# Two-piece loads (120 and 8 rows) for ten early tiles, and a new order of all operations, in a gated linear attention and MLP kernel

## The chip, the cores and the metric

The kernel runs on one core of a Trainium2 chip. The metric is the device time of one execution in microseconds (us). The kernel before takes 165.41 us, the median of three runs between 165.22 and 166.08.

## The reference

The inputs q, k, v and alpha are float32 of shape (4, 8, 768, 48): four batches, eight heads, 768 steps, 48 columns. A recurrence runs over the steps, and its output, with the heads side by side, goes through a mixer with a residual and an MLP with a residual:

```
state = alpha[t][:, None] * state + outer(k[t], v[t])     # for each batch and head
x[t]  = q[t] @ state                                       # x: (4, 768, 384)
u     = x + transpose(transpose(x) @ U @ V)                # U: 768 x 32, V: 32 x 768
out   = u + relu(u @ w_ch1) @ w_ch2                        # w_ch1: 384 x 1536, w_ch2: 1536 x 384
```

## The kernel before

**Attention.** The recurrence is computed in chunks of 128 steps, six for each batch. The logarithm of alpha (written `lt`, on ACT) is summed over the steps by matmuls ("cumulative matmuls", L343 and the lines behind it), exponentiated into `aa` and `ai`, and multiplied into q and k (`rq`, `rk`, L364 and L530, on DVE or POOL). `rv` is a cast of v (L258 on ACT, L262 on POOL). TensorE transposes rk and rq (L377, L543), forms scores (L404, L568), which are masked into `pm` (L415, L578), carries the state on (`st`; L438 are matmuls of rk with rv), and computes the chunk's output into `xb`.

**Two kinds of units.** In batch 0 all six units, and in batch 1 the first four, are *pair* units: two units (halves, of four heads each) share a block of 256 steps. Their tiles are loaded with two neighbouring steps in each partition (L304). The other chunks are loaded by L311. One unit needs four tiles: alpha, k, q and v. A tile is named here by its input, batch (b0), block and half. Every tile of an input, and every tile of 128 x 384 of the weights, has 128 rows and 192 KB.

**Mixer and MLP.** `stage_mix` multiplies by U and V and adds (`ub`) and transposes (`uT`). `mlp1` (L732 on PE, relu on ACT at L742 or on DVE at L744) and `mlp2` (L755 on PE, adding at L762 on DVE, output transfer at L763) follow for each batch. Weights come through `weight` (transfer L277, cast L258 or L262).

**Order.** `Plan.add` records operations with the engines that may run each. `Plan.run` plays them by `TABLE`, three characters for each operation: two for its number and one for its engine (P TensorE, A ACT, D DVE, G POOL, S the queue of SP). `++X` stands for some filler matmuls (L251, on a tile of zeros, into a bank that nothing reads). `SLOTS` names for each operation's new buffers which slot of their pool they take. The order is thus one list, written out beforehand: each engine runs its operations in the list's order and waits only for what they need. All transfers, the outputs' included, are issued on SP, in the list's order, from the `io` pool of 36 tiles. They take eight semaphores in rotation, so transfer n waits until transfer n − 8 has landed. The change's places are these:

```
op.fn({"P": "PE", "A": "ACT", "D": "DVE", "G": "POOL", "S": "SP"}[table[n + 2]])
...
P.add({"SP": 545.0}, lambda e: nc.sync.dma_start(flat(t), src), w=[t])      # weight
```

In the order before, the last tile of batch 0 is v of block 2, half 0, transfer number 25 counting from 0. Sixteen fillers run: 11 ahead of the first cumulative matmul, then 2, 2 and 1 between the first units' cumulative matmuls.

Of the kernel before, what the change touches and what calls it, by code (L numbers as in the profile page):

```python
# [13 lines left out]

CODE = "ABCDEFGHIJKLMNOPQRSTUVWXYZabcdefghijklmnopqrstuvwxyz0123456789+-"
TABLE = """
A8SA4SBESCuA++LCwPBISCYAA+SCyAA9SDbAC1DCaPDyAA5SCxAA7S++CD0PDdPCbAA-SCZGDeAC0DA6SD3ACzAC2PCcACeDC4DCdAC3PC5DBGS++CCnPCoD
BASC6PD2ADfACvACpPDgACfDD1ABMSCgPChPBFSCiAC8DCjDDEABHSBBSDiGCqDC9PC+D++BDkPDGPBDSC-PEHACkPC7DEJPDmABCSBQSDhDDBPBOSDHADAD
DcGBNSDIAClDDJADjPDKDDTPBKSEKABJSDCAELADFGDMPDqPDlDABSDDAEMADLGBPSBLSBSSCmDDrPDOABUSBRSGLADUPDnPDsDDtPDVDDNPDpDAASDoDEOG
DuDDWPGNPCrPDPAGOAEQPDQPGQAENDCsDBTSCtAEPPD5GDXDBVSESADRDDvPBXSERAAeSD7PETPD4GDwADSDGPAD9ADYPADGDxDD6PEVDBYSEWPEBPEIGAGP  # L20
DZDGSGDaDEUDBcSDzAD8AAEPECPAKSAcSAaSGRGEXPD+PGhAEDDAMSGUPAFAGjPAHAEYDEZPGTPGMGACGEADD-DGWAEEPEbDGkAGlAGmAGaPGnGGVDEFAEaD
EGDAfGEcPAISAQSGbDALGGiABWSGXPEdPEeABfSAdGAOSGwPGcDGZDEiPGxDElPEjPAbGEmPGYDErPEsPEkAEoPANGE7PASSEuPGyDE5PBdSHOAGpPAJGEfP
EpPBbSE8DEgPEvPEtDBZSG3AEqAARGHQPAUSExPEnDEzPBaSEhDEwABeSAgSG5PG7AAYSFrPAPGAWSFRPEyDBkSE-PBgSGrAFTPE0DE6DATGFpPHRAAmSFBP
AkSFAAFSDG6ABiSFqAFnPGoDHPGAiSE1PFCAE9PBhSGzDG8AE2DFUDE3PGqPHUDFPPBlSFoAGdGBmSFfPG9GFbPFsAE+DHTAE4DHWPHSAFVPFZPHYDAVGHdP
FQAAuSG4AFWDFgAHGPFcAGsAGePFaDBjSHHDG+GAXGGtPGfDHeDGvDGgDFDPFdPFEAAsSG-PAZAFHPFIAFeDHAPFXPHVDHXPGuDHCAHIGH7AHBDFhPAoSFLP
H9PFYAFMAAqSHfDHlABnSHgDFiAAnGH+AHZDHJDA0SAySFNPHDPAlGAwSA2SFOAHaPBoSHnPHqAAhGH-AFlPHEDFJPBrSHpABwSHoAHFDFjPFFPHrAAjGHbD
HLPFmDHcDHKDG0PFkAHhDHiPHMAHtGIADFGAHNAHvPHjDG1DIBDGGPICPBsSHsGHkAHuPIDPFKDG2AFyPHxAHmGIEAHwDIFAHyPIGPBvSH0DF8PFtPHzDIHD
H1PAvAApGH2DArAAtGGBPH8ABpSH3DH5PFzPIIDF9PA1AAxAA3AH4GIJPGHPH6DGCPIKDAzGILPBySJtAFuPIMAF0PIPPIQDINPGDPB0SIODBxSITPF1DKWA
IVPB8SGIPIRPF2SIWDBtSIUDIbPJvPIcDFvPIZPIaDBqSIXPISAKYPKBAIYDGJDKcABuSKZAF+PKDPIdPKHAJwAGKSFwDBzSCASIeDKbAKrAInPIhPIoDCQS
KaAIfPJyAJ0GB2SIxPKGAJxAGEDIpPIiDKEAIlPJuGB+SIgAF-DKdDIyDKFAB9SKeDJzAImDI-PJ2PKIDI3PB1SKtPIzPLVAI0DB3SKxAJHPB4SI4ACESJFP  # L30
FxSJ4DJAAKCGB5SJ1DB6SJ9PJGDJ+DIjPIqAKuAIkDKJGKRPJ3PIrPJBPLXPKwAKvAKLPKXGKSDNHAI9PB7SJ5DJIDLYAIsDIvPLZAKKPKfPKhDJCAI5PKgP
KNDI+DKMAJNPJOAKTDI6AItPI1PKmPJJPKiDI2AIwAJLPKnDIuDJMACCSI7PJ6PKjPKOPKPDJKAI8ALbGF3PLAACDSKsAKQDJDPOaANJPJ7DKlDF4PB-SKyG
NbAF5PNNAK0PLCPKkDK7PJUPLFALEAJ8DLGAKUPK2DKzDLDAKVDLdPCBSJEDKoGJVPNdPLaGCMSNLANgAJWPGFSNKALIGNfALcPK1PLfDCFSNhALHGJjPLWG
JXDNMALBGKpPJkPK8DK3ACISJ-PNPGLeDNeAGASLJPKqAF6DLKPJPPLgPKADK4PLLDCGSK5DCUSLMALNPOFALODCOSJQPJRPJePLiDLQPLPDJfPF7SK9GJlP
CSSK6DCHSNOGNIANQPLhDNRPJmDLRDOcPLSGOgACRSOHPLTPJSDK+PCNSNjGOfANTDJgPNSALUDOKALjPNiGJZPK-ALkDJTSJaPOeANUPCLSNVDLlPJoPNwA
OIALmAOMGJhDNXPOdALtPOJACXSNWDJpPLvPLpPL1POLANyPLuDNYDLwDN0ACJSLnPJqPLxPLoDONGLqDLzPL2DNkPOiGL0DJnSOvANcALrPJrDJbPLyANZP
NlPLsAN2ANaDNrPNnACVSMJPL3PCKSMFPNzAOxPMKDNsDN1AMHPMNPMGDL4AOhDCPSJcDOzAL-POOPNmAMODMLPMIAMTPMAAMVPOyAOjPCTSMUDNtGL7PNxG
MMDJdSOPPL9PN3DORDOQAL5PO0GL8DOAPMhPMnPMWAOlAL6AN5PMRPOkPCWSMXPL+DOBDN4DNoPOCGMSAOmDMiAMoAOwGOSPOUDOTDOGGMBPMPPMlPO1GMYA
MDPN6PMQANpDN7AO2PMjPMCDMEAJiSObGOVPOYPNqDO4DOWDOXGMZPO3PMkDMmAN8AOqPMaDMuPOrDOZANuPOnPOoDO5AO6POsDN9PN+DMvPMdPMwPMzPN-D
OpDMbPO8DMfPO7DM4PMeDO9PMgAO+AODPNvAOEAOtPM0PMxDOuDNCPO-PMcAM5PM6PPAAPPPPNPPJPJYSPODM1PPHPMpPPQDPKDNDPPRPM2DPBPPIDPCDM9P  # L40
PLPPSDMqPPDPM+PMrPPMDPEDJsSPFPNEPMySM7DP3PPxPPvPPGDMsDPwDPZPPaDPTPP4APlPPpPPdPPjPPUDM3SPeDPVPPyDPfPNFDPWAQBPM-PPXPP-PPkD
PtPPgDPmDPqAP5PPrPPYDPbPQCAPsAP6DP9PPuAPhPQAAPcDPzPPnPP+ANADPiAQIPP7PQSPQDPP1PMtSQNPP8AQEPPoDP0AQXPQFPP2DQGDM8SQJPQKPQcP
QdPNGSQYPQLDQHSQePQOPQZPQMSNBSQPPQfDQaDQgSQTPQUPQQDQVDQbSQRSQWS
"""
SLOTS = """
ABCAADBEAFCABAGAHCDBIACAJABEBBACFAKGAALEBCABDBAMFGNBABBOPCDCBBFQAGADCRSCEBTBCUBBCCDFVCWAADGECBAXYZCAabCBDACDECBGFADBDECD
BcACdAAFBeBfDEAABBFCBBgGAEDAhBCFijACCBBBBEAAGFDACCBCCACEFDADCDACEAGAFGBCAAECFDAGBHEBAIAHCJAKCBLDGMNOFCPEQCRDSBHGATAUABVC
BDWDGXAAFADYZCBHBEBBGCAEaEDCDHBbBCFGBABDHcAGDBAHABBAGdFDeDAfBCBAhgAEBijFHACCAGCEBCCAABADFGCAHBCDCBFDDHACCBBAAGDEFECHABDA
GAGEADFHCBEBDFIFABEJDKCEFLCBDABDMBFCAACQPCBABNBCBATBCDDCGERABAUAAHCCSFEBOCBWVGCCXBYCCAACEHDGCBFDBAAZDBEAHBACDBBGBHBFACGA
bDCBFEHGABACdBDBHCBcDABGCEFACBCCCCGaDCAeADAABBDAfCGABCHBBhFBABECDBCAHFBiAjCEDCBgHCEAACBDADDAFCCDCGAEFCDAABDACDGGBEBACAAC  # L50
DAEABHFGCCBBEEDAHEBBEFACGDBAHCIBFJGBDABCBCHDAHFCGEACCMABCHDBBBFDEGHAACBKFACDEDABCBAAGHBAFCCCHDDAGBBCFEDBHACAGBBDFDEBAAEB
CGFDGADHDBCGAABDGCCAEABCBGEBABFCDGBFCBDECHFGBDECGBCFDHAECBADBDABC
"""


# [21 lines left out]
class Plan:  # L77
# [40 lines left out]
    def run(self, table, slots):  # L118
        nxt = iter(slots)
        for n in range(0, len(table), 3):  # L120
            if table[n : n + 2] == "++":
                for _ in range(CODE.index(table[n + 2])):
                    self.warm()
                continue
            op = self.ops[CODE.index(table[n]) * len(CODE) + CODE.index(table[n + 1])]
            for b in op.bufs:
                if b.slot is None:
                    b.slot = b.pool.slots[CODE.index(next(nxt))]
            op.fn({"P": "PE", "A": "ACT", "D": "DVE", "G": "POOL", "S": "SP"}[table[n + 2]])


def mm(*cols):
# [4 lines left out]
def kernel(  # L137
# [12 lines left out]
    nc = tc.nc  # L150
    B, H, S, D = q.shape
# [21 lines left out]
    P = Plan()  # L173
# [82 lines left out]
    def copy(eng, dst, src):  # L256
        if eng == "ACT":
            nc.scalar.copy(dst, src)  # L258
        elif eng == "DVE":
            nc.vector.tensor_copy(dst, src)  # L260
        else:
            nc.gpsimd.tensor_copy(dst, src)  # L262

    def small():
# [4 lines left out]
        for i in range(2):  # L269
# [2 lines left out]
            P.add({"PE": mm(TW)}, lambda e, vb=vb, sl=sl: nc.tensor.matmul(vb()[:, 0:TW], lhsT=sel.rearrange("r a b -> r (a b)"), rhs=v_bf[:, sl], start=True, stop=True), r=["v_bf"], w=[vb], mode="V")  # L272
            P.add({"DVE": 470, "ACT": 390}, lambda e, vb=vb, sl=sl: copy(e, vm_sb[:, sl], vb()[:, 0:TW]), r=[vb], w=[("vm", i)])

    def weight(dst, src, key, engs):
        t = Buf(io)
        P.add({"SP": 545.0}, lambda e: nc.sync.dma_start(flat(t), src), w=[t])  # L277
        P.add(engs, lambda e: copy(e, dst, flat(t)), r=[t], w=[key])

    def flat(t):  # L280
        return t().rearrange("p h d -> p (h d)")

    def weights1():
# [11 lines left out]
    def paired(b, c):  # L295
        return c // 2 < PAIRS[b]

    def stage_loads(b):
        def load(t, src, c):
            if paired(b, c):  # L300
                hs, sl = slice((c % 2) * HP, (c % 2 + 1) * HP), slice((c // 2) * 2 * C, (c // 2 + 1) * 2 * C)
                P.add(
                    {"SP": 775.0},
                    lambda e: nc.sync.dma_start(  # L304
                        t().rearrange("p (h j) d -> p h (j d)", j=2), src[b, hs, sl, :].rearrange("h (p j) d -> p h (j d)", j=2)
                    ),
                    w=[t],
                )
# [508 lines left out]
```

## Time and profile before

| | us |
|---|---|
| median of three runs | 165.41 |
| profiled execution, whole | 167.33 |
| its span (first to last instruction) | 165.5 |
| around the span | 1.83 |
| PE busy | 156.8 (95%), 1810 matmuls |
| DVE, ACT, POOL busy | 121.5, 90.5, 54.0 |
| transfers on SP | 146, 28.5 MB |

The profile is one execution, and its times are microseconds from the span's start. "PE" is TensorE's matmuls, "PEld" its weight loads, which run beside them. SPq is the time that SP's queue takes to issue a transfer, waiting for a semaphore included. A row of the chain or of the waits names an instruction by output and line, and behind "<-" what released it last.

### The profile page before, as it was taken

How to read it: one execution, taken by the hardware profiler on the slowest of the kernel's cores; microseconds unless marked ns; L12 is line 12 of the kernel's file. 1: busy time of each engine (PE TensorE's matmuls, PEld its weight loads, DVE VectorE, ACT ScalarE, POOL GpSimd, SP SyncE). 2: the span in 40 equal slices, each digit the busy share in tenths (PEclk: the TensorE clock that was granted, in tenths of full speed). 3: DMA queues.
4: the chain of work that ended last, by engine and by line, in shares of the span. 5: the costliest groups of instructions: out<-in, count | busy, mean ns of one | idle time of the engine just before them, and what ended most of it. 6: DMA issues, size and time to landing. Idle time of an engine off the chain costs nothing.

```text
span 165.5 us, 4676 instructions
## 1 busy us (share of the span) xinstructions
PE 156.8 (95%) x1810; PEld 103.0 (62%) x1810; DVE 121.5 (73%) x271; ACT 90.5 (55%) x225; POOL 54.0 (33%) x88
## 2 busy tenths in 40 slices
PE   7897959999999999999999999999999999999991
PEld 2455737666767656667677675766777566566660
DVE  6198957988999817999697887887988285752241
ACT  4598847679497363885876354994724201342000
POOL 7032848439445310422717453364320000000000
PEclk9999996999999999999999999999999999999999
DMA  5999979999989979999999999966000012100133
GB/s 126 279 289 267 255 170 247 279 324 310 260 174 269 286 141 216 195 228 204 199 218 233 210 246 197 223 142 190 0 4 29 18 53 95 46 1 4 48 143 143
DMA packets 87126, 28.81 MB, mean 174 GB/s; under 512 B 80928, under 2 KB 87072, under 8 KB 87104
## 3 DMA queue, kind: packets, MB, share of 16 engines
q1 hardware_dynamic: 87104, 28.52, 69.7%
q8 instruction: 14, 0.23, 0.6%
q14 instruction: 8, 0.07, 0.1%
HBM read 23.79 MB, written 4.72 MB: 172 GB/s over the span
## 4 chain that ended last, share of the span: by engine, by line
PE 78%; SPq 9%; DMA 4%; DVE 3%; issue 1%; ACT 1%; POOL 1%; ACTq 0%
PE ps L755 28%; PE ps L732 27%; SPq L304 9%; DMA io<-in_v_dram 4%; PE ps L543 3%; PE ps L680 2%; PE ps L568 2%; PE ps L701 2%; PE ps L635 2%; PE ps L377 1%; PE ps L510 1%; PE ps L630 1%; PE ps L650 1%; PE ps L591 1%; DVE pm L415 1%
## 5 line engine op out<-in xcount | busy, mean ns | idle before, releaser
L755 PE MATMUL ps<-w_sb,h1t 128*128 128x384 bf16 x288 | 54.0, 326 | 0.0
L732 PE MATMUL ps<-uT,w_sb 128*128 128x384 bf16 x288 | 53.0, 326 | 0.0
L742 ACT ACTIVATE h1t<-ps 128x384 bf16<-128x384 f32 x52 | 23.7, 496 | 28.8 <-PE ps L732 28.3
L755 PEld LDWEIGHTS <-h1t 128*128 128x128 bf16 x288 | 26.2, 97 | 16.2 <-issue 1.2
L732 PEld LDWEIGHTS <-w_sb 128*128 128x128 bf16 x288 | 26.5, 98 | 15.0 <-POOL w_sb L262 0.2
L744 DVE TENSOR_SCALAR h1t<-ps 128x384 bf16<-128x384 f32 x44 | 23.4, 551 | 7.7 <-PE ps L732 7.6
L578 DVE TENSOR_TENSOR pm<-ps,maskc 128x512 bf16<-128x512 f32 x28 | 17.6, 684 | 4.8 <-PE ps L568 3.3
L681 DVE TENSOR_TENSOR ub<-xb,ps 128x384 bf16<-128x384 bf16 x24 | 12.3, 549 | 8.2 <-PE ps L680 8.2
L762 DVE TENSOR_TENSOR ou<-ub,ps 128x384 f32<-128x384 bf16 x24 | 13.1, 549 | 7.0 <-PE ps L755 6.8
L415 DVE TENSOR_TENSOR pm<-ps,maskp 128x512 bf16<-128x512 f32 x20 | 13.3, 685 | 0.2
L262 POOL CAST w_sb<-io 128x384 bf16<-128x384 f32 x18 | 9.1, 517 | 11.5 <-DMA io<-in_moe_w_ch_dram 11.4
L530 POOL TENSOR_TENSOR rk<-io,ai 128x384 bf16<-128x384 f32 x9 | 8.2, 913 | 13.6 <-DMA io<-in_alpha_dram 9.1
L262 POOL CAST rv<-io 128x384 bf16<-128x384 f32 x16 | 8.4, 532 | 12.1 <-DMA io<-in_v_dram 11.1
L530 POOL TENSOR_TENSOR rq<-io,aa 128x384 bf16<-128x384 f32 x9 | 8.5, 952 | 9.3 <-DMA io<-in_q_dram 5.7
L260 DVE CAST xb<-ps 128x192 bf16<-128x192 f32 (+1 forms) x19 | 8.1, 437 | 3.4 <-PE ps L635 2.7
L602 POOL TENSOR_TENSOR st<-sm,tot 128x384 bf16<-128x384 f32 x7 | 6.1, 865 | 13.9 <-DVE sm L618 6.6
L258 ACT COPY qt<-ps 128x512 bf16<-128x512 bf16 x14 | 9.3, 668 | 1.8 <-PE ps L543 1.0
L523 ACT ACTIVATE tot<-ps,off 128x4 f32<-128x4 f32 x22 | 5.7, 278 | 8.2 <-PE ps L512 7.8
L503 ACT ACTIVATE lt<-io 128x384 bf16<-128x384 f32 x14 | 7.4, 530 | 1.6 <-DMA io<-in_alpha_dram 1.6
L258 ACT COPY kt<-ps 128x512 bf16<-128x512 bf16 x12 | 7.1, 590 | 1.1 <-PE ps L377 0.8
L521 ACT ACTIVATE aa<-ps 128x384 bf16<-128x384 f32 x14 | 7.0, 508 | 1.1 <-PE ps L512 1.1
L364 POOL TENSOR_TENSOR rq<-io,aa 128x384 bf16<-128x384 f32 x6 | 5.8, 970 | 5.0 <-ACT rv L258 2.3
(116 smaller groups left out, 252.5 us busy)
## 6 DMA issues: line engine op xcount, KB each, us to landing
io<-in_alpha_dram SPq DMA_DIRECT2D x24, 192.0 KB, 4.2
io<-in_q_dram SPq DMA_DIRECT2D x24, 192.0 KB, 3.7
io<-in_k_dram SPq DMA_DIRECT2D x24, 192.0 KB, 4.1
io<-in_v_dram SPq DMA_DIRECT2D x24, 192.0 KB, 4.0
io<-in_moe_w_ch_dram SPq DMA_DIRECT2D x24, 192.0 KB, 4.6
out_dram<-ou SPq DMA_DIRECT2D x24, 192.0 KB, 2.2
v_in<-in_moe_V_dram SPq DMA_DIRECT2D x1, 96.0 KB, 3.7
u_in<-in_moe_U_dram SPq DMA_DIRECT2D x1, 96.0 KB, 4.8
```

Of the source, the lines that this page charges most:

```text
L258: nc.scalar.copy(dst, src)
L262: nc.gpsimd.tensor_copy(dst, src)
L304: lambda e: nc.sync.dma_start(t().rearrange("p (h j) d -> p h (j d)", j=2), src[b, hs, sl, :].rearrange("h (p j) d -> p h (j d)", j=2)),
L415: nc.vector.tensor_tensor(dst, s2, maskp.to_broadcast([C, 2, 2, C]), op=ALU.mult)
L530: eng.tensor_tensor(dst()[:, :, 0:D], a(), x(), op=ALU.mult)
L578: nc.vector.tensor_tensor(pm()[:, :, par, :], s2, maskc.to_broadcast([C, HP, C]), op=ALU.mult)
L681: P.add({"DVE": 465}, lambda e, c=c, hb=hb: nc.vector.tensor_tensor(ub()[:, c, :], xb()[:, c, :], hb()[:, 0:DM], op=ALU.add), r=[hb] + xk( ...
L732: nc.tensor.matmul(hb()[:, 0:TW], lhsT=w1_sb[:, ct, jt * 128 : (jt + 1) * 128], rhs=u_half(uT, ct, tt, b in QUEUE_U), start=(ct == 0), sto ...
L742: nc.scalar.activation(dst, hb()[:, 0:TW], AF.Relu)
L744: nc.vector.tensor_scalar_max(dst, hb()[:, 0:TW], 0.0)
L755: nc.tensor.matmul(hb()[:, 0:DM], lhsT=h1()[:, jt, c * C : (c + 1) * C], rhs=w2_sb[:, jt, :], start=(jt == 0), stop=(jt == NJ - 1),)
L762: P.add({"DVE": 468}, lambda e: nc.vector.tensor_tensor(ou(), ub()[:, c, :], hb()[:, 0:DM], op=ALU.add), r=[hb, (ub, c)], w=[ou])
```

## The change

`Plan.run` knows two engine letters more: "Q" (ACT) and "X". A load or weight whose letter is X is issued as two transfers, one of rows 0 to 119 and one of rows 120 to 127, one behind the other on SP; with S it is one transfer of 128 rows, as before. `TABLE` and `SLOTS` are replaced throughout.

```diff
-            op.fn({"P": "PE", "A": "ACT", "D": "DVE", "G": "POOL", "S": "SP"}[table[n + 2]])
+            op.fn({"P": "PE", "A": "ACT", "D": "DVE", "G": "POOL", "S": "SP", "Q": "ACT", "X": "SX"}[table[n + 2]])
...
+    def parts(e, dst, src):
+
+        cuts = (0, 120, 128) if e == "SX" else (0, 128)
+        for lo, hi in zip(cuts, cuts[1:]):
+            nc.sync.dma_start(dst[lo:hi], src[lo:hi])
+
     def weight(dst, src, key, engs):
         t = Buf(io)
-        P.add({"SP": 545.0}, lambda e: nc.sync.dma_start(flat(t), src), w=[t])
+        P.add({"SP": 545.0, "SX": 545.0}, lambda e: parts(e, flat(t), src), w=[t])
...
                 P.add(
-                    {"SP": 775.0},
-                    lambda e: nc.sync.dma_start(
-                        t().rearrange("p (h j) d -> p h (j d)", j=2), src[b, hs, sl, :].rearrange("h (p j) d -> p h (j d)", j=2)
+                    {"SP": 775.0, "SX": 775.0},
+                    lambda e: parts(
+                        e, t().rearrange("p (h j) d -> p h (j d)", j=2), src[b, hs, sl, :].rearrange("h (p j) d -> p h (j d)", j=2)
                     ),
```

What the new table holds, counted from it:

| | before | after |
|---|---|---|
| operations on PE, DVE, ACT, POOL | 369, 245, 224, 73 | 369, 234, 236, 72 |
| loads and outputs in one piece, in two | 146, 0 | 136, 10 |
| transfers on SP | 146 | 156 |
| place of the last b0 tile (v, block 2, half 0) | 25 | 31 |
| fillers ahead of the first cumulative matmul | 11 | 8 |
| fillers behind it | 2, 2, 1 | 1, 3, 1, 2, 1 |

The ten tiles in two pieces, in the order of their issue: q b0 block 1 half 0, v b0 block 1 half 1, q b1 block 0 half 0, a tile of w_ch1, alpha b1 block 1 half 0, another tile of w_ch1, q b1 block 0 half 1, q b1 block 1 half 0, a tile of w_ch2, and v b1 block 1 half 1. Lines behind `parts` stand six lines further down.

More of the change, by code (lines that the diff above doesn't have):

```diff
@@ L16 @@
 TABLE = """
[L17 to L40, printed above, removed]
@@ L41 @@
-PLPPSDMqPPDPM+PMrPPMDPEDJsSPFPNEPMySM7DP3PPxPPvPPGDMsDPwDPZPPaDPTPP4APlPPpPPdPPjPPUDM3SPeDPVPPyDPfPNFDPWAQBPM-PPXPP-PPkD
-PtPPgDPmDPqAP5PPrPPYDPbPQCAPsAP6DP9PPuAPhPQAAPcDPzPPnPP+ANADPiAQIPP7PQSPQDPP1PMtSQNPP8AQEPPoDP0AQXPQFPP2DQGDM8SQJPQKPQcP
-QdPNGSQYPQLDQHSQePQOPQZPQMSNBSQPPQfDQaDQgSQTPQUPQQDQVDQbSQRSQWS
+A4SCYABMSBESBASBGSA8SA7SDbADEAA6S++ICaPEHABBS++BDdPCuAA5SCdABQS++DDGPA+SA9SBDSBISA-SCcABFSABSEJPCbAAYSDfABCXBHXDHABNSCfD
+BUSBOSBJSBRSDKDDIABKSBcSBPSDiGCwPBLSBSXCZGAUSBTS++BChPAaSAASCxACjD++CDkPAcSDgACeDDeAAKXGLABYX++BCgPCzADFGCyAAeSBgSDJADmD
@@ new lines @@
+C0DCnPCoDDMPEKACiAAWSASSC2PC1GCpPELADyACkPDhGADGDLGCqDDODCvAAIXDTPDUPBZSCmDD0PEMADVDC9PClDAQSAMSBVSGNPDcGC+DDWPC4AD1AAOS
+C3PC-PBWXDXDD2ADjPC5DBkSAGPAEPDADGOAAqSENGAZAD3AC6PAHDEOGDNPDqPA2SD4GAFAC7DDlAD5GGhADrPDPADnPGRGBeSAgSGPADsDEIGDtPBXSBdS
+C8DDuDGjPAkSGQAGlADpDGSGAmSCrPGMGBaXAwSEQPDoDESADQPDRDD6PCtAEPPAiSD8DBiSGkAA0SDSDAbGDvPERAD7PGTPACGGmADwDDxDEWPCsAETPAoX
+D9AAuSAdGAfGGVDHOAEVDDBPDYPDCAAsSEXPEUDBbSD+PDzADaADZAAJGARGHQPDDAEYDGUPAySEBPD-DGoGGWAEADECPEZPEDDBfXEaDATGGaPEbAEEPGXP
+HRAGbDEGDEFAGcDEcPEdPEfPErPHTAEiPAVAGZDEeAHSAGYDEuPG3AEoPEgPEsPElPEpPEjPAPGEvPEmPE1PEhDG5PEqABhSEkAEwDE3PGdDEnAG8AEtDBmS
@@ new lines @@
+EzPExPHlAFRPFTPArGAhGEyDAXAE4DBlSHUGFSAFUAFPPFhPFnPG7AG+GG6AFjPFrPFJPAjGE0DFlPFoAALAANAG9DFkDFKAHnPFZPFsDE7PFQDE2DE8DAlG
+E-PFmAE9PBjSGnDHrAG-PE+AFNPBnSFVPHoAE5PHBDFiDFODH7AFWAGqPFXPFHPFaDFDPHqAE6DFYAFBPFAABoSHpAHVDAxGFIAFpPGsDAvGHXPApGFqDHZD
+FCAFFPFEDFdPGpPHWPFfPGiABwSA3AFeAFgDHAPGrAB0SFbPFLPHYDGwPA1GFGDHCAFMABpSAnAGePGfAAzGHtDHsGHPGBqSB8SH9PGxDGgDHvPBsSH-AH+A
+GyDFyPBySHxDHaPBtSGtPHDPHbDFcAF8PHFDAtAGBPHEDHcDGvDFzPGCPGuDG4AHmAF0PF1DGDPBvSG0PHGPGEDHdPBrSHuPF2SGzGHHDF9PHeDIBGG1DIAD
+G2AF+PICPIEAIDPHIGHJDH1PHfGHwDF-DIFAHLPHgDHMAHKGH2DHhGHNAGFSHiPH3DH8AIGPHkAJtAHyPKWAIHDFtPF3PB4SKrAF4PH4GH0DIIDIJPHzDJvP
@@ new lines @@
+H5PBxSHjDKYPJwAF5PH6DBuSIKAKZACASKaAJ0DILPGGPIMDF6DJ2PJzAIZPJxAINPKcAKBAFuPJ4DIaDITPIVPJ1DIbPJuGFvPJyAIUDIPPIODKbAIWDKDP
+GHPBzSKCGB5SLVAIXPIYAIQDKtPKFAKuAIRPKxAKEAIcDKHAGIPISDFwDIdPKdGJ3PKvAI1PIeDKwAItPIhPI2ALAAKeDKGACISJ9PJ+DJNPIvPIuDInPLCP
+IpPGJDLEALFAIiDJ5DKgPIwAI9PJJPLDAJDPLGAIoAJKAIzPKiDNHAB3SJEDKIGI+AJHPKJDKXAJLPKRPIjPJMDIqAIxPJODCCSKSDIyDIfPLXPLHGNJPB1S
+I3PI0AJIDNKAIkAKLPB7SB6SKfPIlPI4DIrPKmPLZAIgALYAB+SB2SKhDCBSKNDKTGImDIsAKnDKjPKsAJ6PJPPLJPLBACUSKkDKlDJ7DJQPI5PLLDB9SJBP
+J8DKyGI6AKoDK7PK0PJCANNALIGF7SNLAJFPCESKzGKKPJ-PJGAK2DJRPK8DCVSI-PI7PCDSLKPKpPKMAK9GGASJUPLMDLbGNwAI8ANMAK1PNPGLQPJAAKqA
@@ new lines @@
+JSDJZPLRDK3ALNPLODB-SLPDNOGKAAOvAKOPKPDK4PJVPJaPNQPNRPK5DKQDCQSNTANbALTPLUDJWPLdPLaGJePCMSLfDNIGK6DKUPFxSLcPGKSKVDNyPCGS
+K+PJbPNSDLeANUPK-DLgPJfPJgPLSGJXDOxPN0ALhDLiDJjPCHSLWACWSJhDJcDLjPNXPOyALkAJkPOzALlPNVDOaAO1GLmAOFACFSNdPJlPNcALnPO0DCJS
+NYDLpPLvPN2ALtPNWDLqDLoDN1AJiSJoPNzALuDJpPLrPLzPLwDL1PNeANfAOcPCLSNhANgAO2PLxPOfACRSCOSL2DLsAL0DJqPO3POgACKSL3POdALyDNiG
+O5DL4DL9PNjDOHPNkPMRPO4ANmDMHPL+AOeAMSAMVPNrPNZPOKACNSMjPMWDNsDMFPMPPNaANxAMkAMLPJTSMIAOLACSSNtGOIAOhGNlPOJAMMAJrDJmDN3D
+MGDMXPMhPCTSJsSL5PMDPOAPOMGOiGL6AMiDOBDN4DCPSOGGL-PJYSOCGMJPMQAMYAMNPNnAMKDN5PMEDObAMbPMAAONGNoPO6PMTPMODNpDN7AOkPOOPMcA
@@ new lines @@
+NqDMBPMUAOqPL7PMdPO7DOVPJdSL8AOQAO8DCXSOmDN6POjPMfPMeDOPPOWDORAOlAMpPMCDOXGOwANuPN8DMuPNvAMqPN9PMgDOrDOnPOSPMvPN-DMZPOTD
+OsGMwPO9POUDM9PN+DODPO+AOoDMaAOpDJnSM4POtPOEDOYPOZAMlPOuDMnPO-PMmDPADMrPNCPMoDPHPPNPMsDPJPM5PPKDMtSPPPNDPM+PPBPPIDPODPQD
+PDPMzPPCDM6PPEDPLPPRPPMANEPM-PNFDPFPPSAPvPPGDP9PP+APlPPzPMxDPxPNADM0PPdPM7DPjPPyAP5PPeDM1PP-PP0APkAPfPQAAP1PPgDPmDPTPP2A
+P3PPtPP6DPwAPXPP4AQBPPrPPYAPVPNBSPsDPZPPuAQcPNGSPnPPoAM2DPUDPpPP7PQCDPqAPhPPaDPbPP8DQXPQYPPiAPWAQNPQIPPcAQSPMySQJPQTPQKP
+QZPQDPQdPQUPQePQEPQaDQVDM8SQOPQbSQfDQFPQWSQLDM3SQMSQGDQgSQHSQPPQQDQRS
@@ L44 @@
 """
 SLOTS = """
[L46 to L49, printed above, removed]
@@ L50 @@
-bDCBFEHGABACdBDBHCBcDABGCEFACBCCCCGaDCAeADAABBDAfCGABCHBBhFBABECDBCAHFBiAjCEDCBgHCEAACBDADDAFCCDCGAEFCDAABDACDGGBEBACAAC
-DAEABHFGCCBBEEDAHEBBEFACGDBAHCIBFJGBDABCBCHDAHFCGEACCMABCHDBBBFDEGHAACBKFACDEDABCBAAGHBAFCCCHDDAGBBCFEDBHACAGBBDFDEBAAEB
-CGFDGADHDBCGAABDGCCAEABCBGEBABFCDGBFCBDECHFGBDECGBCFDHAECBADBDABC
+AABCDEFGBCHAAIBBJAKCLMNOPAQDARBSTBUAVWXYACZabBEcdAefFgCAGhBBBiCjACBAACDBCFBAEAADBGCBACFDABCFABHAEABDFIEGADCCCJGKACCMDBBN
+BDGEBFDLABACBBDCGCOPCDEQRDSCBCATFEAVUBAAGACABWCXAZEAACBBGDEYBbBACFABCadEFDDCGcCBBCBAAfEFCGABCCAECGAFAAAHCBEDAAgCDhBFBHEA
@@ new lines @@
+eDAGFCCCBHEABBCHEAGAACBDjEBGAABFDEHCBAGDFAACBDHCDGCFFEBCBBIHDBBCBHiGDAEAABEKCCDBHBAGCFBCAEDAGGADBBHEJCABAADBHAAGBCCDABBA
+CFADECHABABGMACBFDANECOBPCBHCBDFBABHDCABGFCACDEQERBGBHAAFACCADDABGFBBCBLDDHGEDFBCBBCBABGDAAVACABEAGBWBFECHSACDUXBCGAABTb
+BYDCABFADECGDaCAACZBBAFDCCCGdBAEBBcBDgGFABACACDCHCDGABBCBfDBFDAHEBCChAAFHBCACCDFHeECADFBECCABBBjBCABECAAGACBABDDDEAFBACD
+GCFCAHEBCGIADCBEiCEHHACDACCEHBCDAAAGECJHBAGAEEGDBBHCADDFBNDCEAAABKAAABDBGBECFHBACCAGDEFHCBBCMCAGHDBABCCCBBEDGAABHFAGCBHF
+DBHAGBDABGBAADACDBACDACBCDBGBBEDDAFHEBDFEBDGCHEDBDCAFGEBCAFCBACBD
```

## The prediction

> **What bounds the kernel now.** I read the page first (busy times, then the slices), then the windows, what PE waited for, the chain that ended last, and SP's timeline.
>
> From the page, busy time of each engine and of PE over 40 slices of 4.14 us:
>
> ```profile
> PE 156.8 (95%) x1810; PEld 103.0 (62%) x1810; DVE 121.5 (73%) x271; ACT 90.5 (55%) x225; POOL 54.0 (33%) x88
> PE   7897959999999999999999999999999999999991
> PEclk9999996999999999999999999999999999999999
> PE 78%; SPq 9%; DMA 4%; DVE 3%; issue 1%; ACT 1%; POOL 1%; ACTq 0%
> ```
>
> PE is busy 95% of the span, and every slice that is not full lies in the first seven, apart from the last. The last row is the chain: PE carries it, except for SP's queue (9%) and one transfer (4%). The change leaves all 1810 matmuls in place, so time can only move at the start, in gaps between matmuls, or at the granted clock.
>
> The windows (length, then busy us and count for PE, PEld, DVE, ACT, POOL; then granted clock, DMA share, GB/s):
>
> ```profile
> 0.00:5.00 5.00, 3.81 (x9) 1.35 (x10) 2.48 (x26) 2.33 (x3) 3.15 (x15) 1.00 0.58 141
> 5.00:10.00 5.00, 4.50 (x55) 2.90 (x54) 2.45 (x5) 3.27 (x11) 0.58 (x1) 1.00 1.10 293
> 10.00:15.00 5.00, 4.61 (x96) 3.23 (x94) 4.63 (x11) 4.92 (x15) 1.42 (x2) 1.00 1.08 290
> 15.00:20.00 5.00, 3.98 (x96) 3.04 (x96) 4.58 (x12) 3.81 (x12) 3.37 (x4) 1.00 1.01 252
> 20.00:25.00 5.00, 3.13 (x75) 2.19 (x73) 3.19 (x8) 2.79 (x8) 2.68 (x5) 1.00 0.74 175
> 25.00:30.00 5.00, 4.94 (x107) 3.52 (x106) 4.16 (x11) 3.43 (x10) 3.16 (x5) 0.66 1.00 261
> 50.00:60.00 10.00, 9.75 (x152) 6.63 (x150) 8.00 (x17) 6.19 (x15) 4.05 (x7) 1.00 0.92 245
> 160.00:165.50 5.50, 2.10 (x13) 1.07 (x11) 1.66 (x3) 0.00 (x0) 0.00 (x0) 1.00 0.38 143
> ```
>
> PE's idle time: 1.19 us at the start, then 0.50, 0.39, 1.02 and 1.87 from 5 to 25 us (3.78 together), 0.25 from 50 to 60, and 3.40 at the end (last adds and the output's transfer; the change leaves their number and order of size alone). At 20 to 25 us the transfers also slacken: 0.74 and 175 GB/s between 252 and 261. At 25 to 30 PE is full but at a mean clock of 0.66: it was granted 0.5 from 26.07 to 29.48.
>
> What PE waited for (total, times, longest):
>
> ```profile
> PE ps L438 <- ACT rv L258: 1.8, 1, 1.8
> PE ps L377 <- DVE rk L364: 1.0, 1, 1.0
> PE ps L343 <- ACT lt L334: 0.5, 1, 0.5
> ```
>
> and the chain's longest piece in the first 60 us (start, length):
>
> ```profile
> 17.46 6.58 DMA io<-in_v_dram
> ```
>
> The longest wait is for rv, the cast of the last tile of batch 0 (v, block 2, half 0). ACT had nothing to wait for but that tile: its transfer, number 25 counting from 0, was issued at 17.46 and took 6.58 us, where the mean v tile takes 4.0 from issue to landing.
>
> SP's timeline there (start, length):
>
> ```profile
> 19.10 2.03 SPq L304 DMA_DIRECT2D io<-in_k_dram  x1
> 21.18 0.55 SPq L265 DMA_DIRECT2D u_in<-in_moe_U_dram  x1
> 21.77 2.23 SPq L304 DMA_DIRECT2D io<-in_v_dram  x1
> ```
>
> An issue takes 0.50 to 0.55 us, but some take 2 us: there are eight semaphores in rotation, and number 33 is held until number 25 has landed (21.77 + 2.23 = 24.00; it landed at 24.04). In the first 60 us such holding adds some 15 us over 22 issues. So SP is slowed by landings, not by its own work, and the landings are the thing to look at. Each transfer counts sixteen marks as its shares land. Number 25 had fifteen by 22.20 and its sixteenth at 24.04: 1.84 us for one share. Number 24 shows 20.41 and 21.73, number 26 shows 22.73 and 24.46. These lags follow 16384-byte packets of the instruction queue q8 (at 13.28, 22.01 and 27.15 us, 0.93 to 1.49 us each): code for the engines is fetched by the channel that one share uses too.
>
> **The change part by part.** It has two parts, which can't be summed apart, because the new order is made for the split transfers.
>
> *The split.* Ten tiles (seven pair tiles and three weight tiles) come as 120 and 8 rows. 128 rows in sixteen shares are 8 rows each; 120 rows are fifteen such shares, and if they take the first fifteen, the sixteenth, the lagging one, gets none of the ten transfers. Its service of a pair tile took 0.53 to 0.57 us in the trace (marks at 15.33, 15.86, 16.41, 17.00), so it is spared ten of these, about 5.4 us, of some 9 us by which it is held up by code packets up to 60 us. In a sentence apart: the Trainium skill ("DMA: Bandwidth & Descriptors", section "Why a DMA increments its semaphore by 16 and not by 1") says that such a transfer uses the largest number up to sixteen that divides its rows, on the lowest-numbered engines, by which 120 rows leave the last engine out; no run here shows a 120-row transfer.
>
> Its price is on SP: 146 transfers become 156, ten more issues at 0.55 = 5.5 us. They go past every later load. The cover is the held-up time: 15 us in the first 60. But cover needs holding to come after each split, and the two pieces also take two of the eight places in the rotation, one of them for a sixteenth of the bytes. Bounds: nothing if all is covered; 6 × 0.55 = 3.3 us if nothing is, for the six splits ahead of the point from which PE is continuously busy (q b0, v b0, q b1, w1, alpha b1, w1). I take +0.1, near the covered end, since the transfers ahead of 26 us are already spaced by landings of 0.6 to 0.65 us a tile, slower than an issue.
>
> *The new order: early waits.* The last tile of batch 0 goes from place 25 to place 31 in SP's order: ahead of it come four whole tiles more (w1, two of alpha b1, one of k b1) and the two small pieces of split tiles. At the 0.59 us at which tiles land, 6 × 0.59 = 3.5 us later; without the 1.84 us of lag, 1.7 later. That tile is no longer awaited by the same work, though: in the changed order units of batch 1 stand ahead of the last unit of batch 0, whose tiles came before it. The first complete unit (four tiles) lands at place 9 instead of 8, 0.6 us later, and eight fillers instead of eleven run before the first cumulative matmul (3 × 0.43 = 1.3 us less), so the first stretch isn't simply better. What PE can do by 25 us is set by how many tiles have landed, and the same tiles at the same pace give the same sum of waits. I take 0 for the 3.78 us, bounds −1.85 (the rv wait gone, with nothing late behind it) and +1.7.
>
> *The half-speed stretch.* From 26.07 to 29.48 us matmul groups are longer than elsewhere: L377's four 0.60 against 0.40, L490's sixteen 0.50 against 0.37, L477's four 0.53 against 0.34. That is about a third of 3.41 us, less what PE would have waited, 0.9 us. It comes once in the execution, right behind PE's emptiest window (3.13 of 5 us). If the waits lie spread over several places, I expect no such stretch: −0.9, bounds 0 and −1.7 (half of 3.41).
>
> *Late waits.* At 53.22 PE waits 0.4 us behind rq (L530), and at 57.56 0.15 for a w2 tile; both follow landings late by 1.0 to 2.5 us (number 68: fifteenth mark 54.50, last 56.98). With the lagging share ahead by 5.4 us they go: −0.4, bounds −0.55 and −0.25 (the window's idle time).
>
> *Edits at nothing.* One matmul-mode switch more (64 against 63) is 0.1 us, inside every rounding. ACT takes 12 operations more and DVE 11 fewer; they are busy 55% and 73%, and if this cover were gone, 12 × 0.5 = 6 us would have to lie on the chain, where ACT has 1%. The same sixteen fillers run, before PE's first full stretch in both.
>
> Sum: 0 − 0.9 − 0.4 + 0.1 = −1.2. The profiled execution took 167.33 us (a span of 165.5 and 1.83 around it), so 166.1; it lies 1.92 above the median of 165.41, so the median comes to 164.2.
>
> **The rivals.**
>
> *SP becomes the bound (slower).* The chain from 0.74 to 17.46 us is SP's issues throughout: up to there SP, not the landings, is last. Every piece issued early pushes the whole list back 0.55 us. Two splits stand ahead of the last tile of batch 0 (1.1 us), six ahead of the full stretch (3.3 us); half of the latter covered gives +1.6 without the other gains, 167.0. For it: this chain, and issues without holding at 14.67 to 18.55 us. Against it: DMA share over 1.00 from 5 to 20 us, so tiles issued sooner wouldn't land sooner. It decides if the issue of an 8-row piece takes 0.5 us or more and v b0 block 2 half 0 lands after 25.5 us. In a sentence apart: the Trainium skill, same page, "Rules for kernel authors", says not to split a transfer over partitions, since both parts use the same engines, and to use one of 128; whole 128-row transfers lagging by one sixteenth speak against it here, the SP chain for it. Chance 0.25.
>
> *The lagging share is not the one left out.* Nothing in the trace says which of the sixteen marks belongs to the code packets' channel. If it is among the fifteen, or if 120 rows aren't dealt so, the split does nothing but cost its issues, and the order built on it meets late tiles: the last tile of batch 0 is 1.7 us later than hoped, of which PE pays most: +1.5, 166.9. Chance 0.12.
>
> *All is hidden.* The waits are bound elsewhere (the half-speed stretch comes again and the early sum is unchanged): −0.4 + 0.2 = −0.2, 165.2. For it: 95% busy PE with the same matmuls. Chance 0.18.
>
> **How the numbers follow.** The forecast, 164.2, has 0.45. Its own range is 162.6 (early waits −1.6 on top) to 165. The range for 8 in 10 is 162.6 to 167.2: it reaches over both slower cases' values and leaves out the far ends of the price on SP and of the waits. A measurement here can tell about 0.5%, 0.8 us. Faster by more than that: 0.40 of the forecast's 0.45 and 0.04 of the hidden case, 0.44. Within: 0.05 + 0.12 + 0.04 of the slower cases, 0.21. Slower: the rest, 0.35.
>
> **What would show it.** Right: 120-row transfers with all marks within 0.3 us of one another at 20 to 25 us; clock 1.00 from 25 to 30; PE idle of 5 to 25 us within 3 to 4.5; SP's held-up time down by about the 5.5 us that its new issues take. Wrong: idle time from 5 to 25 us above 5 us with SP's issues ahead of it in the chain (first rival); a late sixteenth mark within the 120-row transfers (second); a half-speed stretch anywhere (third). A late gap above 0.5 us after 50 us would overturn the late term.

## The result and the profile after: 1.3% slower

The changed kernel takes 168.36 us in the median of four runs (167.28 to 169.86), beside 165.75 for the kernel before (165.22 to 167.86). The ratio is 1.0129, with a 95% interval of 1.0081 to 1.0177: about 2.1 us slower, where 1.2 us faster was forecast. 165.41 times the ratio is 167.5, just beyond the upper end of the range (167.2). The profiled execution of after took 169.86 us (a span of 168.1) and is the slowest of the four; the ratio leaves it out. It shows where time went in that execution; the sizes are taken from the experiments.

The page of after, busy times, PE and its clock over 40 slices, and the chain:

```profile
PE 157.6 (94%) x1810; PEld 102.8 (61%) x1810; DVE 118.5 (70%) x260; ACT 93.5 (56%) x237; POOL 55.1 (33%) x87
PE   7969899997969999999999999999999999999991
PEclk9999879999999999999999999999999999999999
PE 70%; DMA 17%; SPq 7%; POOL 2%; issue 1%; DVE 1%; ACT 1%; POOLq 0%
```

The chain has moved. Transfers held 4% of it and now hold 17%; SP's own queue fell from 9% to 7%. PE's slices (4.2 us each) show new holes at the tenth and twelfth places, at 38 to 42 and 46 to 50 us, where the kernel before had none; its windows there:

```profile
30.00:40.00 10.00, 10.00 (x98) 6.78 (x97) 8.43 (x18) 7.97 (x20) 5.85 (x12) 1.00 1.05 306
40.00:50.00 10.00, 10.00 (x152) 6.59 (x150) 9.68 (x23) 7.90 (x21) 5.49 (x10) 1.00 0.93 229
```

The windows of after (same columns as before):

```profile
5.00:10.00 5.00, 4.42 (x51) 2.79 (x49) 0.85 (x2) 3.89 (x11) 0.62 (x1) 1.00 1.13 306
10.00:15.00 5.00, 3.75 (x65) 2.28 (x65) 4.60 (x10) 4.61 (x15) 2.72 (x5) 1.00 1.11 309
15.00:20.00 5.00, 4.18 (x78) 2.99 (x78) 4.30 (x11) 3.96 (x11) 4.08 (x6) 0.94 0.99 245
20.00:25.00 5.00, 5.00 (x113) 3.83 (x112) 4.12 (x10) 4.12 (x12) 3.59 (x5) 0.72 0.98 261
25.00:30.00 5.00, 5.00 (x150) 3.76 (x145) 4.60 (x11) 3.99 (x13) 2.21 (x4) 1.00 0.74 198
30.00:40.00 10.00, 8.91 (x72) 5.46 (x70) 7.17 (x15) 6.98 (x19) 2.03 (x4) 1.00 0.98 262
40.00:50.00 10.00, 8.24 (x67) 5.04 (x65) 7.51 (x16) 6.38 (x15) 6.41 (x10) 1.00 1.02 274
50.00:60.00 10.00, 9.78 (x168) 6.61 (x168) 8.37 (x18) 4.01 (x11) 5.67 (x10) 1.00 0.93 198
```

PE's idle time from 5 to 30 us is 2.65 us, less than before (3.84). From 30 to 60 us it is 1.09 + 1.76 + 0.22 = 3.07 us, where before it was 0.25. The half-speed stretch is there again, 3.41 us long, at 19.4 to 22.8 us; in it PE is full, as it was in the stretch before. PE's busy time rose from 156.8 to 157.6; the stretch, as long as before, doesn't explain that, and no run here does. The difference of the spans, 2.6 us, is −1.2 (early waits) + 2.8 (30 to 60 us) + 0.8 (PE busier) + 0.2 (the end).

What PE waited for, and the chain between 29 and 56 us (start, length):

```profile
PE ps L383 <- DVE h1t L750: 1.4, 1, 1.4
PE ps L251 <- DVE filler L184: 1.2, 1, 1.2
PE ps L383 <- DVE rk L370: 0.9, 1, 0.9
PE ps L738 <- ACT w_sb L258: 0.9, 1, 0.9
```

```profile
29.87 3.94 DMA io<-in_moe_w_ch_dram
34.58 5.62 DMA io<-in_q_dram
...
40.42 1.00 POOL rq L370
41.44 4.15 DMA io<-in_moe_w_ch_dram
45.65 5.34 DMA io<-in_moe_w_ch_dram
51.05 5.03 DMA io<-in_k_dram
```

L738 is mlp1 of batch 0: it waited 0.9 us for a tile of w_ch1 (place 45 in the order of tiles) that landed at 38.49. The wait of 1.4 us ends at 48.69. The view names a relu on DVE, but POOL's rq ended at the same time (48.63): it ran from 47.72, after 1.40 us of waiting for the q tile of place 58, which landed at 47.50. The 5.62 us are a q tile in two pieces, issued at 34.58 and landed at 40.20; POOL's rq waited for it, and three weight casts waited behind rq. Part of these waits is one late share: the tile of place 45 has its fifteenth mark at 36.52 and its last at 38.49, and the 120 rows of the q tile have theirs at 39.02 and 40.20, both behind a packet of the instruction queue q8 at 35.22.

### The profile page after: what moved, and what is told of

It is laid out like the page before. It is cut to its first block, busy times and chain, and to the rows that moved or that the text cites. A ratio compares the mean times of both kernels' runs of the same rounds, so it can differ in the third digit from the quotient of the medians.

```text
span 168.1 us, 4683 instructions
## 1 busy us (share of the span) xinstructions
PE 157.6 (94%) x1810; PEld 102.8 (61%) x1810; DVE 118.5 (70%) x260; ACT 93.5 (56%) x237; POOL 55.1 (33%) x87
## 4 chain that ended last, share of the span: by engine, by line
PE 70%; DMA 17%; SPq 7%; POOL 2%; issue 1%; DVE 1%; ACT 1%; POOLq 0%
PE ps L761 26%; PE ps L738 21%; DMA io<-in_moe_w_ch_dram 8%; SPq L279 6%; PE ps L549 4%; DMA io<-in_q_dram 3%; DMA io<-in_k_dram 3%; DMA io<-in_v_dram 3%; PE ps L574 2%; PE ps L707 2%; PE ps L686 2%; PE ps L641 2%; PE ps L496 2%; PE ps L383 1%; PE ps L636 1%; PE ps L516 1%
## 5 line engine op out<-in xcount | busy, mean ns | idle before, releaser
L738 PE MATMUL ps<-uT,w_sb 128*128 128x384 bf16 x288 | 52.5, 326 | 0.9 <-ACT w_sb L258 0.9
L738 PEld LDWEIGHTS <-w_sb 128*128 128x128 bf16 x288 | 26.8, 98 | 16.6 <-ACT w_sb L258 1.2
L748 ACT ACTIVATE h1t<-ps 128x384 bf16<-128x384 f32 x57 | 26.9, 500 | 14.4 <-PE ps L738 14.2
L750 DVE TENSOR_SCALAR h1t<-ps 128x384 bf16<-128x384 f32 x39 | 20.5, 551 | 11.0 <-PE ps L738 10.9
L536 POOL TENSOR_TENSOR rk<-io,ai 128x384 bf16<-128x384 f32 x10 | 9.4, 952 | 8.0 <-DMA io<-in_k_dram 4.0
L258 ACT CAST xb<-ps 128x192 bf16<-128x192 f32 (+1 forms) x21 | 7.8, 387 | 6.7 <-PE ps L641 6.3
L258 ACT CAST rv<-io 128x384 bf16<-128x384 f32 x14 | 7.3, 530 | 6.0 <-DMA io<-in_v_dram 6.0
L258 ACT COPY qt<-ps 128x512 bf16<-128x512 bf16 x10 | 6.6, 662 | 6.4 <-PE ps L383 3.4
L526 ACT ACTIVATE ai<-ps 128x384 bf16<-128x384 f32 x14 | 6.9, 500 | 4.8 <-PE ps L518 4.8
L260 DVE COPY qt<-ps 128x512 bf16<-128x512 bf16 x14 | 7.4, 531 | 2.7 <-PE ps L549 1.9
L262 POOL CAST rv<-io 128x384 bf16<-128x384 f32 x10 | 5.3, 536 | 11.6 <-DMA io<-in_v_dram 11.1
L258 ACT COPY uT<-ps 128x768 bf16<-128x768 bf16 x4 | 3.1, 798 | 9.6 <-PE ps L707 9.6
```

Source lines behind the costliest of these rows:

```text
L536: eng.tensor_tensor(dst()[:, :, 0:D], a(), x(), op=ALU.mult)
L738: nc.tensor.matmul(hb()[:, 0:TW], lhsT=w1_sb[:, ct, jt * 128 : (jt + 1) * 128], rhs=u_half(uT, ct, tt, b in QUEUE_U), start=(ct == 0), sto ...
L748: nc.scalar.activation(dst, hb()[:, 0:TW], AF.Relu)
L750: nc.vector.tensor_scalar_max(dst, hb()[:, 0:TW], 0.0)
```

## The experiments

All ratios are to the kernel before, measured beside each kernel on the same chip, with 95% intervals.

**Order and split apart.** Two kernels: the changed order without splits, and the order before with the same ten splits.

```diff
# order alone: after, TABLE with the ten letters X set to S
# split alone: after's code with before's TABLE and SLOTS, the same ten loads set from S to X
```

> The changed kernel with all ten split loads put back into one transfer of 128 rows each; order, engines and buffers are the changed ones (146 transfers). Theory I (the ten extra issues on SP make it slow): ratio to before at or below 1.000, that is at least 1.5 us faster than the changed kernel (1.013). Theory L (the split leaves out the wrong share, so it neither costs nor helps, and the new order meets late tiles): within 0.5% of the changed kernel, 1.008 to 1.018, with PE idle from 30 to 50 us of 2 to 3.5 us as after the change. Theory S (the split helps, but the order loses more than it gives): slower than the changed kernel by 0.5% or more, over 1.018.

> The kernel before, in its own order and buffers, with the same ten tiles issued in two pieces of 120 and 8 rows (156 transfers). Theory I: 1.006 to 1.013, from 1 to 2 us slower than before, with SP's issues longer in the chain. Theory L: 0.997 to 1.004, and the late mark after the code packets of q8 stays in the 120-row transfers (1 us and more). Theory S: below 0.996.

Measured: order alone 1.0036 (1.0003 to 1.0068, median 166.19), split alone 1.0101 (1.0051 to 1.0151, median 167.81). So the ten splits cost about 1.0% (1.7 us) in the old order and 0.9% (1.5 us) in the new one (1.0129 against 1.0036), and the new order gains nothing by itself. Theory L put the split at nothing and the whole loss on the order, and falls; S falls; theory I gave the right size for the split alone, and put the order alone a little too low.

Order alone, windows:

```profile
15.00:20.00 5.00, 4.01 (x82) 2.92 (x81) 4.28 (x11) 3.78 (x11) 3.87 (x5) 1.00 1.03 268
30.00:40.00 10.00, 10.00 (x85) 6.56 (x83) 8.39 (x18) 8.07 (x21) 4.10 (x7) 1.00 1.00 290
40.00:50.00 10.00, 10.00 (x146) 6.66 (x144) 8.60 (x20) 8.87 (x22) 5.87 (x11) 1.00 1.10 322
```

With the same order and buffers, PE has no idle time from 30 to 50 us, and 290 and 322 GB/s land there instead of 262 and 274. The tile of place 45 lands at 34.67 instead of 38.49, place 58 at 43.73 instead of 47.50, place 73 at 54.70 instead of 59.85. Of the 3.8 us at place 45, 1.7 are the late share (0.26 us between the last two marks in order alone, 1.97 after); at place 73 it is only 0.3 of 5.2. The old order with splits shows the same kind of wait, in one profile:

```profile
PE ps L738 <- POOL w_sb L262: 1.1, 1, 1.1
```

**The cut.** The changed kernel, with `cuts` changed.

```diff
-        cuts = (0, 120, 128) if e == "SX" else (0, 128)
+        cuts = (0, 112, 128) if e == "SX" else (0, 128)     # also (0, 126, 128) and (0, 64, 128)
```

> The changed kernel with the cut at row 112 instead of 120: the same ten tiles, the same 156 transfers and order, but 112 rows are sixteen shares of seven, so no share should be left out, and 16 rows are sixteen of one. Theory L: the same as the changed kernel within 0.4% (1.009 to 1.017), as leaving out one share did nothing there. Theory S: slower than the changed kernel by 0.5% or more. Theory I: the same as the changed kernel (same number of issues). The marks of the large pieces should number sixteen, without one that comes with the issue.

> The changed kernel with the cut at row 126: 126 rows as fourteen shares of nine, and 2 rows as two. It asks which share the code packets delay: with the cut at 120 the late mark stayed in the large piece. If it is the fifteenth, the large pieces show no mark over 0.8 us late behind q8's packets, and by theory L the time falls by 0.3 to 1 us against the changed kernel (1.007 to 1.011). If it is one of the first fourteen, late marks of 1 to 2 us stay and the time is as after the change or, since each share has nine rows instead of eight, up to 0.5 us longer (1.012 to 1.017).

> The changed kernel with the cut at row 64: two pieces of 64 rows, sixteen shares of four rows each, as many issues as after the change. The cut at 112 (sixteen and sixteen shares) came out at 1.021 and the cut at 120 (fifteen and eight) at 1.013. If the number of shares or the sixteenth share is what costs there: 1.017 to 1.024. If it is the smallness of the second piece (one row for each share): 1.009 to 1.016.

Measured: 1.0210 (1.0159 to 1.0261) at 112, 1.0122 (1.0082 to 1.0161) at 126, 1.0350 (1.0296 to 1.0404) at 64. With the number of transfers the same, two pieces of sixteen shares each cost more than 120 and 8, and two equal ones most of all. At 64 the transfers ran dry:

```profile
15.00:20.00 5.00, 3.79 (x81) 2.81 (x79) 3.93 (x11) 3.12 (x8) 3.03 (x4) 1.00 0.67 160
```

160 GB/s beside the 268 of order alone. The expectation for 64 had the sixteen shares at 1.017 to 1.024; they don't explain 1.035. Two things go with it. SP's issue of the two pieces of a tile takes longer: 0.69 us in the median at 126, 0.71 at 120, 0.90 at 112 and 1.23 at 64, where a whole one of these ten tiles takes 0.43 in order alone; the losses over order alone (0.9, 0.9, 1.7 and 3.1%) rise in the same order. And all six runs at 64 have a mean clock of 0.960 to 0.987: some 8 us at half speed in the mean run, which at the 0.8 to 0.9 us that 3.41 us of it cost (see the half-speed stretch below) is about 2 us, an estimate. How much each makes stays open.

At 112 the large pieces show sixteen marks with their data, as expected, but 1.021 lies above the ranges of theories I and L; it lies in that of S alone, which the order alone rules out. At 126 the time lies in the range for a late share among the first fourteen, though the interval reaches into the other range. The marks decide: at place 48 the last mark of the 126 rows is 0.72 us late, as those of its whole neighbours (0.59 and 0.56), so leaving out two shares doesn't leave out the late one either.

**Which splits.** The first three of the ten, or the last seven, the others whole.

```diff
# first three: TABLE of after, the last seven letters X set to S; last seven: the first three set to S
```

> The changed order with only the first three of the ten splits (q b0 block 1 half 0, v b0 block 1 half 1, q b1 block 0 half 0, all issued before 23 us); the other seven tiles are whole. Known so far: the order without splits 1.004 of before, with ten splits 1.013. If the price is paid where PE first runs short of tiles (the prediction's place, ahead of the last tile of batch 0), this is 1.009 or more. If it is paid from 25 us on, where SP's issues lie back to back and wait for buffers, this is within 0.4% of the order alone, 1.000 to 1.007, with no PE wait from 30 to 50 us.

> The changed order with only the last seven splits (issued from 25 us on); the first three tiles are whole. If the price is paid from 25 us on: 1.009 to 1.015, with PE waits of 1 us or more in sum from 30 to 50 us and the tiles of places 63 to 73 landing 3 us or more later than in the order alone. If it is paid early: 1.001 to 1.007.

Measured: 1.0088 (1.0059 to 1.0116) and 1.0136 (1.0090 to 1.0183). Both come out above the order alone, the first with intervals that touch, so neither place alone is the answer, and the two prices over 1.0036 (0.5% and 1.0%) add up to more than that of all ten (0.9%). The first lies between its two ranges. The second lies in the range for a price paid from 25 us on, but without that range's signs: in its profile PE is idle for 0.24 us from 30 to 50, and place 73 lands 1.9 us later than in order alone, not 3 or more.

**An extra transfer without a split.** The ten tiles whole, and behind each a tiny transfer that nothing reads.

```diff
     def parts(e, dst, src):
-        cuts = (0, 120, 128) if e == "SX" else (0, 128)
-        for lo, hi in zip(cuts, cuts[1:]):
-            nc.sync.dma_start(dst[lo:hi], src[lo:hi])
+        nc.sync.dma_start(dst, src)
+        if e == "SX":
+            nc.sync.dma_start(tiny.pop(), q[0, 0, 0:8, 0:24])     # twice; or nc.scalar; or X on ten later loads
```

> The changed order with all ten tiles loaded whole (128 rows), and behind each of them an extra transfer of 8 rows of 96 bytes of q into a small tile that nothing reads: an eleventh issue without moving any row of the tile. If the price is the issue on SP and its place in the rotation: as after the change, 1.009 to 1.016. If it is that the rows of a split tile are dealt to fewer shares, with the tile's bytes landing later: as the order alone, 1.000 to 1.007.

> As the kernel with ten tiles whole and ten extra tiny transfers (1.012 of before), but the tiny transfers are issued on ACT's queue: SP issues 146 transfers again, while the ten tiny ones still take their places in the rotation of eight semaphores. If SP's issue time is the price: 1.000 to 1.007, as the order alone (1.004), up to 0.5% more if ACT's ten issues of some 0.4 us delay what waits for ACT. If the place in the rotation is the price (one of eight transfers in flight carries next to nothing): 1.009 to 1.016.

> The changed order, the ten tiles whole, and two tiny transfers (8 rows of 96 bytes each, read by nothing) behind each of them instead of one: 166 transfers. The price of an extra transfer doubled. The order alone is 1.004, with ten tiny transfers 1.012. If each extra transfer on SP costs its issue there: 1.017 to 1.026, with SP's issues from 25 to 50 us covering 3 us more. If ten already cost all there is to lose (a place taken from what is in flight, given back by the buffers): 1.010 to 1.016.

> The changed order, all tiles whole, and ten tiny transfers behind ten loads of the places 76 to 95, issued from some 54 to 70 us on, instead of behind the ten tiles of the change. If the price depends on the stage (tiles awaited soon up to 50 us, none awaited later): 1.000 to 1.007, as the order alone. If an extra transfer costs the same anywhere: 1.009 to 1.016.

Measured: ten tiny transfers 1.0123 (1.0046 to 1.0200), twenty 1.0166 (1.0107 to 1.0224), ten behind later loads 1.0015 (0.9982 to 1.0048), ten issued by ACT 1.0124 (1.0078 to 1.0169). An extra transfer costs as much without moving a row of any tile; where no tile is awaited soon it costs nothing that can be measured. Twenty came out above ten, but the intervals overlap and 1.0166 falls between the two expected ranges, so whether the price doubles stays open. The price of the ten isn't the half-speed stretch: the four runs that their ratio uses all have a mean clock of 0.997 or more. The row of twenty, where 213 GB/s land:

```profile
15.00:20.00 5.00, 4.02 (x79) 2.81 (x73) 4.30 (x10) 3.67 (x9) 3.72 (x6) 1.00 0.84 213
```

In this window the rate falls with what has been added ahead of it, in one profile each: 268 (order alone), 268 (last seven splits) and 285 (late tiny ones), with nothing added; 256 with tiny transfers behind two tiles and 213 with twice as many; 245, 237, 233 and 160 with the cuts at 120, 126, 112 and 64. With the tiny ones on ACT it is 266, after 249 in the window ahead, where order alone has 297.

Where PE pays is less clear than the profile of after suggests. It has 2.85 us of idle time from 30 to 50 us; other profiles have less there at about the same price: 0.22 (ten tiny), 0.24 (last seven splits), 0.52 (cut at 126), 1.12 (split alone). What the costly ones share in the changed order is that tiles land later:

| changed order with | tile of place 73 lands at, us | ratio |
|---|---|---|
| ten tiny transfers, late | 54.33 | 1.0015 |
| nothing added | 54.70 | 1.0036 |
| ten tiny transfers | 56.37 | 1.0123 |
| cut at 126 | 57.34 | 1.0122 |
| twenty tiny transfers | 57.69 | 1.0166 |
| cut at 112 | 59.09 | 1.0210 |
| cut at 120 (after, the execution of 169.86) | 59.85 | 1.0129 |
| cut at 64 | 62.29 | 1.0350 |

This alone doesn't tell cause from effect, since work that runs late also frees its buffers late, and SP waits for these (after, for 3.4 us behind POOL's casts of weights alone).

The ten on ACT were to tell SP's issue time from the place in the rotation, and don't: ACT reaches them at other times than SP its tiles, and SP waited for them:

```profile
SPq L277 <- DMA tiny<-in_q_dram: 1.4, 2, 1.0
```

**Fewer issues on SP.** The kernel before, with the transfers of U and V issued by ACT.

```diff
-        P.add({"SP": 450.0}, lambda e: nc.sync.dma_start(u_in, moe_U...), w=["u_in"])
+        P.add({"SP": 450.0}, lambda e: nc.scalar.dma_start(u_in, moe_U...), w=["u_in"])     # and v_in
```

> The kernel before, with its two small transfers (U and V, 96 KB each, places 23 and 29 on SP) issued on ACT's queue at the same point of the order: two issues fewer on SP ahead of 22 us, same places in the rotation. If SP's issue time is the price: 0.993 to 0.998 (three extra issues at that stage cost 0.5% in the changed order). If the rotation or the transfers themselves are the bound there: 0.998 to 1.003.

Measured: 1.0022 (0.9989 to 1.0055). Two issues taken off SP ahead of 22 us and put on ACT bring nothing, which speaks against SP's issue time as the bound at that stage of the kernel before.

No version came out faster than the kernel before.

## Why the prediction was wrong, step by step

**Both parts were put too low.** The prediction had the split at −0.3 us (price +0.1, late waits −0.4) and the order at −0.9 (early waits 0, half-speed stretch −0.9). Measured were +1.5 for the splits in the new order and +0.6 for the order alone (1.0036): together the 3.3 us between −1.2 and 2.1.

**The term that failed first: the price of ten more transfers, taken as +0.1 us.** It measured 1.5 us in the new order and 1.7 in the old, within the bounds given (0 to 3.3). What failed is the step from "SP is held up for 15 us" to "so ten issues are covered". Each 8-row piece was indeed cheap on SP, 0.29 to 0.38 us and once 0.55, 3.5 us for all ten. But the held-up time was no free time. The prediction read SP's 2.23 us at 21.77 as the rotation of eight: number 33 waiting for number 25. Counted again in the same trace, that transfer is number 30, and number 22, eight ahead of it, had landed at 19.58. What ended the holding was number 25, five ahead. Of the first 38 transfers of the kernel before, each whose issue took over 0.6 us ended with four or five transfers not yet fully landed, and in all of these but the very first the one eight places ahead had landed 2.4 to 4.6 us earlier. So there the queue takes some four or five transfers, and SP stands until there is room. It is no fixed number: from 30 to 34 us, with many weight tiles among them, up to seven were under way without holding. That an 8-row piece takes such room from a whole tile is argued from these counts and from the falling rate; what exactly counts as room was not settled. Nor is SP's own issue time ruled out as the price: it grows with the loss over the four cuts. Ten tiny transfers on ACT, with no issue on SP, cost as much, which speaks against it, but SP waited for them.

The rotation itself came to bind only with the pieces. SP's waits for a transfer, 20 to 60 us, after the change:

```profile
SPq L279 <- DMA io<-in_moe_w_ch_dram: 1.5, 5, 0.5
SPq L279 <- DMA io<-in_q_dram: 0.8, 1, 0.8
SPq L317 <- DMA io<-in_moe_w_ch_dram: 0.3, 1, 0.3
SPq L279 <- DMA io<-in_k_dram: 0.3, 1, 0.3
```

That is 2.9 us; order alone has 0.5 and the kernel before 0.2. But ten tiny transfers cost as much with 0.2 us of such waits, so this is not the price by itself.

**The share that was to be left out.** Half right. A piece of 120 rows shows fifteen marks with its data and one right behind its issue, a piece of 8 rows eight with its data; this agrees with the Trainium skill ("DMA: Bandwidth & Descriptors", section "Why a DMA increments its semaphore by 16 and not by 1"). From 12 to 16 us whole tiles lag by 0.43 to 0.63 us in one share, and the 120 rows of q b0 block 1 half 0 don't (15.94 and 15.95): a mild laggard is left out. The long lags are another share's. Behind q8's packet of 15.25 (1.06 us) the 120 rows of v b0 block 1 half 1 have their last two marks at 17.22 and 18.00. Behind q8's packet of 27.02 (1.83 us) a whole tile has its last two marks at 28.03 and 30.23, the 120 rows issued next at 28.57 and 30.78, and their 8 rows at 28.75 and 28.84. So what these packets delay is among the fifteen and not among the eight. That they are the only cause isn't shown: in the kernel before, the late mark of number 24 came at 21.73, ahead of the packet of 22.01. The second rival's mechanism was true, at a chance of 0.12; its price was not what decided, as the tiny transfers show.

**Early waits, taken as unchanged.** In after 2.65 us against 3.84, in order alone 4.26, and in the same order with late tiny transfers 2.71. One profile doesn't give this term to better than 1.5 us, more than the whole forecast.

**The half-speed stretch, −0.9.** Its size was right: of the runs that its ratio uses, order alone takes 166.69 in the mean where the mean clock is under 0.995, and 165.76 where it is above; the kernel before beside it 166.38 and 165.60. That it would go was wrong. Nor was there much to gain at the median: the term was read from the profiled execution, which has the stretch, and carried over to the median of 165.41, while most runs of the kernel before have none. All four runs of after have a mean clock under 0.995; order alone has it in 8 of 12 runs, the same order with late tiny transfers in 2 of 12, the kernel before in 17 of 68. Without the stretch order alone lies 0.16 us above the kernel before, so most of the order's +0.6 is probably this stretch coming more often, in few runs. It doesn't follow PE's emptiest window, as the prediction had it: after, PE's emptiest window is 10 to 15 us, and the stretch begins at 19.4. So the forecast sign of a clock of 1.00 from 25 to 30 us came true by luck. No edit here is shown to remove it.

**Late waits, −0.4.** The opposite came: 3.07 us of idle time from 30 to 60 us in the profile of after, against 0.25; only 0.22 of it lies behind 50 us. The step assumed that transfers run further ahead of PE by then; they fell 3.8 us behind those of order alone at place 45 and 5.2 at place 73. And the share that was to be spared still lagged, by 1.97 us at place 45.

**The rivals.** The first, SP as the bound (chance 0.25), had the sign and, with 167.0 us, the value nearest to what came (167.5). Its own signs failed: v b0 block 2 half 0 landed at 23.91, not after 25.5, and an 8-row piece took 0.32 us in the median, not 0.5. In the profile of after the loss falls between 30 and 50 us, on weights and q tiles. Whether the bound is the transfers under way or SP's issuing no experiment here separates. The Trainium skill's rule ("Rules for kernel authors" of the same page) not to split a transfer over partitions agrees with every run here: 120 and 8, 126 and 2, 112 and 16, and 64 and 64 rows all lose.

## What to carry to other kernels

Before counting a queue's waiting time as cover, find which event ends it: if it is the landing of what is under way, an added transfer isn't covered by it. Cost an added transfer by a kernel that adds only it (here a tiny one that nothing reads) at the place in question; ten of them cost 0.9% in the first 50 us (1.0123 against 1.0036), later nothing measurable. Before taking a gain off a median, check that the runs at the median have what is to go. And before counting on leaving out a slow share, look at several lags: here they belong to two different shares.

## What the runs showed of the hardware

Two equal halves of 64 rows cost far more than 120 and 8 (1.035 against 1.013), with as many transfers and bytes; SP took 0.62 us in the median to issue a half, 0.39 for 120 rows and 0.32 for 8. One execution of the kernel with the first three splits had a mean granted clock of 0.563 and took 259.38 us, where its other eleven runs lie between 165.93 and 167.34.
